# Four tokens to a partition for the keys and queries of two tiles, and a changed opening, in a sliding-window attention and feed-forward kernel

## The chip, the cores and the metric

The kernel runs on one core of a Trainium2 chip. The metric is device time in microseconds (us), the median of the runs; lower is better. The core has a matrix engine (TensorE, PE in the profile, with its weight loads as PEld), a vector engine (VectorE, DVE), a scalar engine (ScalarE, ACT), a general engine (GpSimd, POOL), and a queue engine (SyncE, SP). They work through their own instruction lists in order and wait for each other with semaphores. Transfers between the large memory and the on-chip memory (SBUF) run on 16 DMA engines; here SP, ACT and POOL issue them. TensorE writes to eight PSUM banks, from which VectorE and ScalarE read.

## What is computed

Eight batches of 576 tokens with 8 heads of 64 numbers go through attention in a window of 32 tokens to either side; the result, 4608 tokens of 512 numbers, goes through two dense layers with an activation between them:

```python
scores = scale * np.matmul(q, k.transpose(0, 1, 3, 2))
mask = np.abs(pos[:, None] - pos[None, :]) <= 32
attn = softmax(np.where(mask, scores, -1e9))
x = np.matmul(attn, v).transpose(0, 2, 1, 3).reshape(4608, 512)
h = x @ w_in                                  # 512 x 2048
g = h * (1.0 / (1.0 + np.exp(-1.702 * h)))
out = g @ w_out                               # 2048 x 512
```

Inputs and output are float32; inside, the kernel works in 16 bits.

## The kernel before

The 4608 tokens are taken as one row of 36 units of 128 queries, four units to a tile of 512, nine tiles in all. The queries are shifted by 32 tokens against the keys, so that a unit needs three blocks of 64 keys and two blocks of 64 queries. The transposed keys stand in `kT`, a ring of 1024 tokens; the transposed queries in `qT`, two tiles of four units.

`scores(u)` makes 24 products of 64 keys against 64 or 128 queries into two PSUM banks, and one exp on ScalarE turns all 1024 columns into `p`. In the first tile a negative mask is added on TensorE beforehand (two products of 128x512); later units are masked by VectorE after the exp (`band`). `values(u)` multiplies `p` with the values, which VectorE or POOL first copies with a shift of 64 tokens into `vo` (`odd_v`), `norm(u)` divides by the sums, and `x_T(u)` transposes the result into `xT` for the dense layers.

The order of the work is written out by hand: each engine executes its instructions in the order of the calls. `head()` does the first tile (units 0 to 3), the dense layers of these units (`layer1`, `layer2`), and the attention of unit 4 to 6; `pairs()` does units 7 to 11; from then on `step(T)` handles one tile at a time in a fixed order (`STEP`, `FIRST`). In `head()` all loads stand ahead of the computation, so POOL issues them in this order as fast as it can; it converts float32 to 16 bits on the way. Three loads (the first 128 keys and the first two units of queries) go through SP as float32, and VectorE and ScalarE round them (`load_raw`, `round_raw`).

Keys and queries of tiles 0 to 2 are loaded by `load_units` (L148): a partition holds one token, 8 heads of 64 numbers each, one transfer for each unit of 128 tokens and each batch that it touches. `transpose_units` makes four 128x128 products from each unit, and `put_units` copies the PSUM bank into `kT` (VectorE) or `qT` (ScalarE). For tile 1 `both_T` (L215) does two units of keys and queries in one double bank, between products of the second layer; for tile 2 `units_T` does the same between products of the first layer. From tile 3 on other functions do this, which stay as they are.

`keep_busy(n, kind)` (L579) issues n products of 128x256 on zeros into the named bank; nobody reads their result. It stands where TensorE would otherwise be idle. A bank named "o", "t", "h" or "i" exists once, "d" is a double bank and exists twice; a write to a bank waits until its last reader is done.

Of the kernel before, what the change touches and what calls it, by code (L numbers as in the profile page):

```python
# [33 lines left out]
class _Kernel:  # L34
# [110 lines left out]
            yield at - lo, b, s, m  # L145
            at += m

    def load_units(self, c, i, units, half=None):  # L148

        if (c, i) not in self.stage:  # L150
            tag, bufs = (("c2", 2), ("qs", 2), ("qs", 2))[i] if c == "q" else (("gs3", "gs1", "gs2")[i], 1)
            self.stage[c, i] = self.work.tile([128, 4, self.H, self.D], BF16, name=c + "s", tag=tag, bufs=bufs)
        src = {"q": self.q, "k": self.k}[c]
        for u in units:
            for n, (off, b, s, m) in enumerate(self.pieces(512 * i + 128 * u + (32 if c == "q" else 0), 128)):
                if half in (None, n):
                    self.nc.gpsimd.dma_start(self.stage[c, i][off:off + m, u], src[b, :, s:s + m, :].rearrange("h s d -> s h d"))

    def load_keys(self, i, units=range(4)):

# [45 lines left out]
            eng.tensor_copy(to, src)  # L206


    def units_T(self, c, i, units, kind, eng, n=128):

        tp = self.bank(kind, [128, len(units), 4, n], BF16, "tp")
        self.transpose_units(c, i, units, tp, n)
        self.put_units(c, i, units, tp, eng, n)

    def both_T(self, i, units, engs):  # L215

        tp = self.bank("d", [128, 2, 2, 4, 128], BF16, "tp")
        for n in range(2):
            self.transpose_units("kq"[n], i, units, tp[:, n])
        for n in range(2):  # L220
            self.put_units("kq"[n], i, units, tp[:, n], engs[n])

    def transpose_units(self, c, i, units, tp, n=128):
        for a, u in enumerate(units):
            for hp in range(4):
                self.nc.tensor.transpose(tp[:, a, hp, :], self.stage[c, i][:n, u, 2 * hp:2 * hp + 2, :], self.ident[:n, :n])  # L226

    def put_units(self, c, i, units, tp, eng, n=128):
        u, m = units[0], len(units)
        if c == "q":  # L230
            to = self.qT[:, :, i % 2, u:u + m]
        else:
            at = (512 * i + 128 * u) % RING
            to = self.kT[:, :, at:at + n * m].rearrange("r a (u p) -> r a u p", u=m)
        self.cast(eng, to, tp.rearrange("r u a p -> r a u p"))

    def load_raw(self, c, u, queue):
# [4 lines left out]
        queue.dma_start(raw, src[0, :, s0:s0 + 128, :].rearrange("h s d -> s h d"))  # L242

    def round_raw(self, c, u, eng):
        self.load_units(c, 0, ())
        self.cast(eng, self.stage[c, 0][:, u], self.stage.pop((c, "raw", u)))

    def scores(self, u, neg=None):
        nc = self.nc
        both, two = self.double("sc")  # L250
        for eo in range(2 if neg is not None else 0):
            nc.tensor.matmul(two[eo], self.ident, neg.rearrange("p h b s -> p (h b s)"), start=True, stop=False)
        sc = [t.rearrange("p (b s) -> p b s", s=SQ) for t in two]
        qT = self.qT[:, :, u // 4 % 2, u % 4].rearrange("r h (b s) -> r h b s", s=SQ)
        for hp in range(4):
            for chunk in range(3):
                lo, blks = 64 * (chunk % 2), slice(max(chunk - 1, 0), min(chunk, 1) + 1)
                at = 64 * (2 * u + chunk) % RING
                for eo in range(2):
                    r = slice(eo * 64, eo * 64 + 64)  # L260
                    nc.tensor.matmul(sc[eo][lo:lo + 64, 2 * hp + blks.start:2 * hp + blks.stop, :], self.kT[r, hp, at:at + 64],  # L261
                                     qT[r, hp, blks],
                                     start=neg is None and hp == 0 and chunk < 2, stop=hp == 3 and chunk > 0)
        p = self.work.tile([128, 2, 8, SQ], BF16, name="p", tag="p", bufs=4)
        nc.scalar.activation(p.rearrange("p e b s -> p e (b s)"), both, AF.Exp, scale=self.scale)  # L265
        self.p[u] = p

    def band(self, u, parts=2):
# [317 lines left out]
    def head(self):  # L586

        nc, dve, act, pool = self.nc, self.nc.vector, self.nc.scalar, self.nc.gpsimd
# [2 lines left out]
        act.copy(self.spark, self.spark)  # L591
        self.load_raw("k", 0, nc.sync)
        self.load_raw("q", 0, nc.sync)
        self.load_raw("q", 1, nc.sync)
        self.setup()
        self.load_units("q", 0, ())
        for u in (1, 2):
            self.load_units("k", 0, (u,))
        self.setup_mask()
        for m in range(3):  # L600
            self.load_v(m)
        self.load_units("k", 0, (3,))
        for u in (2, 3):
            self.load_units("q", 0, (u,))
# [32 lines left out]
        self.units_T("k", 0, (0,), "h", dve)  # L637
# [64 lines left out]
        run(2)  # L702
        self.band(4)
        self.scores(5)
        run(2)
        self.band(5)
        self.values(4)
# [41 lines left out]
    def pairs(self):  # L749

        nc, dve, act, pool = self.nc, self.nc.vector, self.nc.scalar, self.nc.gpsimd

        def run(lst, n=1):
            for _ in range(min(n, len(lst))):
                lst.pop(0)()
# [205 lines left out]
```

## Time and profile before

| | |
|---|---|
| median of 3 runs | 293.88 us (293.29 to 294.08) |
| profiled execution | 294.34 us, of which the span of the profile is 292.6 us |
| TensorE busy | 280.1 us (96%) |
| VectorE, ScalarE, POOL busy | 200.4, 201.9, 131.3 us |
| first run of first-layer products starts | 22.74 us |
| transposes of tile 1, of tile 2 | from 40.16 us, from 58.09 us |
| packets of POOL's loads | 114,208 |

The profile shows one execution. A line of its timeline gives the start, the duration, the engine, the source line, the operation, what it writes and reads with the shapes, how many there are, and in brackets how long the engine sat idle before it and what released it. A line of the windows gives for a stretch of time the length, the busy time and number of instructions of PE, PEld, DVE, ACT and POOL, the share of full speed that TensorE's clock was granted, the share of DMA, and GB/s.

### The profile page before, as it was taken

How to read it: one execution, taken by the hardware profiler on the slowest of the kernel's cores; microseconds unless marked ns; L12 is line 12 of the kernel's file. 1: busy time of each engine (PE TensorE's matmuls, PEld its weight loads, DVE VectorE, ACT ScalarE, POOL GpSimd, SP SyncE). 2: the span in 40 equal slices, each digit the busy share in tenths (PEclk: the TensorE clock that was granted, in tenths of full speed). 3: DMA queues.
4: the chain of work that ended last, by engine and by line, in shares of the span. 5: the costliest groups of instructions: out<-in, count | busy, mean ns of one | idle time of the engine just before them, and what ended most of it. 6: DMA issues, size and time to landing. Idle time of an engine off the chain costs nothing.

```text
span 292.6 us, 8655 instructions
## 1 busy us (share of the span) xinstructions
PE 280.1 (96%) x3601; PEld 225.4 (77%) x3601; DVE 200.4 (68%) x410; ACT 201.9 (69%) x303; POOL 131.3 (45%) x195
## 2 busy tenths in 40 slices
PE   5899999999999999999999999999999999999994
PEld 3568855786866768888788888888888788888884
DVE  2565426888848569777887787778767877737742
ACT  2475616689595779768976897689768975756830
POOL 8975789877772388359239618602100000000000
PEclk9799999999999999999999999999999999999999
DMA  9999999999999999999999999982503020300223
GB/s 138 156 196 204 162 186 156 209 174 120 157 116 151 128 157 134 125 151 156 227 119 161 199 167 139 132 148 90 74 0 145 20 58 0 147 0 2 80 102 108
DMA packets 158310, 37.26 MB, mean 127 GB/s; under 512 B 148544, under 2 KB 154176, under 8 KB 158272
## 3 DMA queue, kind: packets, MB, share of 16 engines
q0 software_dynamic: 114208, 17.97, 95.7%
q1 hardware_dynamic: 41984, 15.21, 32.1%
q10 hardware_dynamic: 2080, 3.54, 3.6%
q8 instruction: 28, 0.46, 0.7%
q14 instruction: 10, 0.08, 0.1%
HBM read 36.70 MB, written 9.44 MB: 158 GB/s over the span
## 4 chain that ended last, share of the span: by engine, by line
PE 72%; ACT 16%; DVE 6%; issue 2%; DMA 2%; SPq 0%; ACTq 0%
PE h_ps L424 28%; PE o_ps L495 20%; PE h_ps L335 8%; PE o_ps L347 7%; ACT p L265 7%; ACT g L430 3%; PE pv L294 3%; ACT L265 2%; PE tp L226 2%; DMA q_raw<-in_q_dram 2%; ACT L577 2%; DVE vo L206 2%; PE sc L261 2%; DVE x L307 1%; DVE p L278 1%
## 5 line engine op out<-in xcount | busy, mean ns | idle before, releaser
L424 PEld LDWEIGHTS <-w_in_s 128*128 128x128 f16 x448 | 42.7, 98 | 9.8 <-issue 2.9
L430 ACT ACTIVATE g<-h_ps 128x512 f16<-128x512 f32 x49 | 29.2, 595 | 28.4 <-PE h_ps L424 26.7
L495 PEld LDWEIGHTS <-g 128*128 128x128 f16 x448 | 43.4, 98 | 5.2
L265 ACT ACTIVATE p<-sc 128x1024 bf16<-128x1024 f32 x36 | 35.3, 1029 | 4.8 <-PE sc L261 4.5
L424 PEld LDWEIGHTS <-w_in_sb 128*128 128x128 f16 x336 | 32.6, 98 | 7.3 <-issue 0.6
L186 POOL DMA_DIRECT2D qu<-in_q_dram x30 | 24.0, 813 | 30.9 <-DMA qT<-qu 28.9
L495 PEld LDWEIGHTS <-gs 128*128 128x128 f16 x336 | 32.8, 98 | 4.2
L459 DVE TENSOR_TENSOR c<-h_ps,c 128x512 f32<-128x512 f32 x28 | 19.2, 686 | 22.8 <-PE h_ps L424 19.8
L196 POOL DMA_DIRECT2D ve<-in_v_dram x40 | 34.0, 869 | 0.4 <-PE pv L294 0.4
L430 ACT ACTIVATE g<-c 128x1024 f16<-128x1024 f32 (+1 forms) x35 | 34.0, 970 | 0.0
L424 PE MATMUL h_ps<-xT,w_in_s 128*128 128x256 f16 x224 | 33.6, 272 | 0.0
L424 PE MATMUL h_ps<-xT,w_in_sb 128*128 128x256 f16 x224 | 32.4, 272 | 0.3
L347 PE MATMUL o_ps<-w_out_sb,g 128*128 128x512 f16 x128 | 32.6, 380 | 0.0
L424 PE MATMUL h_ps<-xs,w_in_s 128*128 128x256 f16 x224 | 31.8, 272 | 0.6
L206 POOL COPY vo<-ve 64x264 int32<-64x264 int32 x49 | 22.1, 451 | 21.8 <-PE pv L294 15.6
L495 PE MATMUL o_ps<-w_out_s,g 128*128 128x256 f16 x224 | 31.5, 273 | 0.0
L335 PE MATMUL h_ps<-xT,w_in_sb 128*128 128x256 f16 x256 | 30.1, 273 | 0.6 <-DVE xT L129 0.6
L495 PE MATMUL o_ps<-w_out_s,gs 128*128 128x256 f16 x224 | 29.5, 272 | 0.0
L164 POOL DMA_DIRECT2D ks<-in_k_dram x27 | 22.8, 860 | 14.1 <-PE h_ps L424 4.8
L335 PEld LDWEIGHTS <-w_in_sb 128*128 128x128 f16 x256 | 24.3, 98 | 3.8 <-DVE xT L129 0.8
L495 PE MATMUL o_ps<-w_out_sb,g 128*128 128x256 f16 x224 | 26.6, 273 | 0.0
L337 ACT ACTIVATE g<-h_ps 128x512 f16<-128x512 f32 x32 | 18.9, 596 | 10.3 <-PE h_ps L335 10.3
(88 smaller groups left out, 473.8 us busy)
## 6 DMA issues: line engine op xcount, KB each, us to landing
ve<-in_v_dram POOLq DMA_DIRECT2D x32, 128.0 KB, 6.3
ks<-in_k_dram POOLq DMA_DIRECT2D x31, 128.0 KB, 7.1
out_dram<-o_sb SPq DMA_DIRECT2D x6, 512.0 KB, 2.9
out_dram<-o_sb ACTq DMA_DIRECT2D x6, 512.0 KB, 3.7
out_dram<-o_sb SPq DMA_DIRECT2D x9, 256.0 KB, 5.4
qu<-in_q_dram POOLq DMA_DIRECT2D x18, 128.0 KB, 7.3
w_out_sb<-in_moe_w_out_dram POOLq DMA_DIRECT2D x4, 512.0 KB, 8.8
w_in_sb<-in_moe_w_in_dram POOLq DMA_DIRECT2D x3, 512.0 KB, 8.2
```

The source lines that it names most:

```text
L164: self.nc.gpsimd.dma_start(ks[off:off + n], self.k[b, :, s:s + n, :].rearrange("h s d -> s h d"))
L186: self.nc.gpsimd.dma_start(qu[off:off + n], self.q[b, :, s:s + n, :].rearrange("h s d -> s h d"))
L196: self.nc.gpsimd.dma_start(self.ve[m % NV][off:off + n, :, :self.D], self.v[b, :, s:s + n, :].rearrange("h s d -> s h d"))
L206: eng.tensor_copy(to, src)
L265: nc.scalar.activation(p.rearrange("p e b s -> p e (b s)"), both, AF.Exp, scale=self.scale)
L335: nc.tensor.matmul(hps[:, i, :], self.w_in_sb[:, kr, ff * 128:(ff + 1) * 128], xT[:, kr, :], start=(i == 0 and kr == 0), stop=(i == 1 and ...
L337: nc.scalar.activation(g[:, 2 * d:2 * d + 2, :], hps, AF.Gelu_apprx_sigmoid)
L347: nc.tensor.matmul(o_ps, g[:, ff, s * 128:(s + 1) * 128], self.w_out_sb[:, ff, :], start=(ff == 0), stop=(ff == self.NFF - 1))
L424: nc.tensor.matmul(ps[:, i, :], a[:, kr, (2 * j + i) * 128:(2 * j + i + 1) * 128], x[:, kr, :], start=first and i == 0 and kr == 0, stop=i ...
L430: act.activation(out, src, AF.Gelu_apprx_sigmoid)
L459: dve.tensor_add(c22, ps, c22)
L495: nc.tensor.matmul(out, a[:, kb, p * 128:p * 128 + 128], b[:, kb, :], start=first and n in (0, 2 * two) and kb == 0, stop=n in (3, 3 - 2 * ...
```

## The change

Keys and queries of tiles 1 and 2 are loaded with four neighbouring tokens to a partition, so that a row of 4 x 64 numbers of one head is moved at once; a tile takes two transfers for keys and two for queries, since it touches two batches. Each head and each of the four tokens is then transposed by itself, 128x64, into the lower or upper half of a bank. The copy into `kT` puts the keys back in the order of the tokens; the queries stay in the order (token within four, group of four), `scores` picks them with a stepped pattern, and the exp restores the order of its columns. The 64 keys that unit 3 needs from tile 1 are loaded by themselves (`load_edge`, `edge_T`).

In the opening the second unit of queries is no longer loaded by SP but by POOL, second in its queue; POOL's first shift of values moves ahead of a weight load; there are more idle products; and the order of some transposes, products and shifts is another. Two transposes in `pairs()` change places.

```diff
-    def load_units(self, c, i, units, half=None):
...
+    def load_units(self, c, units):
...
+    def load_heads(self, i, c, heads=None):
+        key = (c, i)
+        if key not in self.stage:
+            tag, bufs = ("qs", 2) if c == "q" else (("gs1", "gs2")[i - 1], 1)
+            self.stage[key] = self.work.tile([128, self.H, JT * self.D], BF16, name=c + "s", tag=tag, bufs=bufs)
+        lo, hi = heads or (0, self.H)
         src = {"q": self.q, "k": self.k}[c]
...
+        for off, b, s, m in self.pieces(512 * i + (32 if c == "q" else 0), 512):
+            self.nc.gpsimd.dma_start(self.stage[key][off // JT:(off + m) // JT, lo:hi, :],
+                                     src[b, lo:hi, s:s + m, :].rearrange("h (p j) d -> p h (j d)", j=JT))
...
+    def heads_T(self, c, i, hps, kind, eng):
+        tp = self.bank(kind, [128, len(hps), JT, 128], BF16, "tp")
+        for a, hp in enumerate(hps):
+            for j in range(JT):
+                for t in range(2):
+                    self.nc.tensor.transpose(tp[64 * t:64 * t + 64, a, j, :],
+                                             self.stage[c, i][:, 2 * hp + t, j * self.D:(j + 1) * self.D], self.ident)
+        to = slice(hps[0], hps[-1] + 1)
+        if c == "q":
+            self.cast(eng, self.qT[:, to, i % 2], tp)
+            return
+        at = 512 * i % RING
+        self.cast(eng, self.kT[:, to, at:at + 512].rearrange("r a (p j) -> r a p j", j=JT), tp.rearrange("r a j p -> r a p j"))
...
+    def load_edge(self):
+        self.stage["edge"] = self.work.tile([64, self.H, self.D], BF16, name="edge", tag="x", bufs=5)
+        self.nc.gpsimd.dma_start(self.stage["edge"], self.k[0, :, 512:576, :].rearrange("h s d -> s h d"))
...
     def scores(self, u, neg=None):
...
+        mixed = 4 <= u < 12
+        if mixed:
+            qT = self.qT[:, :, u // 4 % 2].rearrange("r h j (b s) -> r h b j s", s=16)
+            b0 = u % 4 * 2
...
-                                     qT[r, hp, blks],
+                                     qT[r, hp, b0 + blks.start:b0 + blks.stop],
...
+        if mixed:
+            nc.scalar.activation(p.rearrange("p e b (r j) -> p (e b) r j", j=JT),
+                                 both.rearrange("p e (b j r) -> p (e b) r j", j=JT, r=16), AF.Exp, scale=self.scale)
...
     def head(self):
...
-        self.load_raw("q", 1, nc.sync)
         self.setup()
-        self.load_units("q", 0, ())
-        for u in (1, 2):
-            self.load_units("k", 0, (u,))
+        self.load_units("q", ())
+        self.load_units("k", (1,))
+        self.load_units("q", (1,))
+        self.load_units("k", (2,))
...
-        self.load_units("k", 1, (0,), 0)
+        self.load_edge()
         self.load_v(3)
         self.load_w_in(0, 1)
+        self.load_w_in(1, 2)
         self.load_v(4, 0)
-        self.load_w_in(1, 2)
+        self.odd_v(2, pool)
         self.load_w_in(2, 4)
-        self.odd_v(2, pool)
...
-        self.load_units("k", 1, (0,), 1)
-        self.load_units("q", 1, (0,))
         for c in "kq":
-            self.load_units(c, 1, (1,))
-        for u in range(2, 4):
-            for c in "kq":
-                self.load_units(c, 1, (u,))
+            self.load_heads(1, c)
...
-        for u in range(4):
-            for c in "kq":
-                self.load_units(c, 2, (u,))
+        for c in "kq":
+            self.load_heads(2, c)
...
-        self.keep_busy(2, "o")
-        self.units_T("q", 0, (0,), "o", act)
-        self.keep_busy(2, "i")
-        self.units_T("k", 0, (1,), "t", dve)
-        self.round_raw("q", 1, act)
-        self.keep_busy(2, "i")
+        self.keep_busy(6, "o")
+        self.units_T("q", (0,), "o", act)
+        self.keep_busy(4, "i")
+        self.units_T("k", (1,), "t", dve)
+        self.units_T("q", (1,), "h", act)
+        self.keep_busy(3)
         self.scores(0, self.neg)
-        self.units_T("k", 0, (2,), "h", dve)
-        self.units_T("q", 0, (1,), "o", dve)
-        self.keep_busy(3, "t")
+        self.units_T("k", (2,), "o", dve)
+        self.keep_busy(5, "t")
+        self.scores(1, self.neg)
         self.odd_v(0, dve)
-        self.scores(1, self.neg)
+        self.keep_busy(2, "t")
         self.values(0, "ot")
         self.odd_v(1, dve)
         self.norm(0)
-        self.keep_busy(2, "h")
+        self.keep_busy(4, "h")
         self.values(1, "hh")
-        self.units_T("q", 0, (2,), "d", act)
-        self.units_T("k", 0, (3,), "d", dve)
+        self.keep_busy(2)
+        self.x_T(0, "o", act)
+        self.units_T("k", (3,), "d", dve)
+        self.units_T("q", (2,), "d", act)
         self.norm(1)
-        self.x_T(0, "o", act)
+        self.keep_busy(2, "o")
         self.scores(2, self.neg)
-        self.units_T("q", 0, (3,), "t", act)
-        self.units_T("k", 1, (0,), "o", dve, 64)
+        self.units_T("q", (3,), "t", act)
+        self.edge_T("o", dve)
...
-        run(6)
-        self.both_T(1, (0, 1), (dve, act))
-        run(1)
-        self.both_T(1, (2, 3), (dve, act))
+        run(5)
+        for hps in ((0, 1), (2, 3)):
+            self.heads_T("k", 1, hps, "d", dve)
+            self.heads_T("q", 1, hps, "d", act)
+            run(2)
         for m in (4, 5):
             self.odd_v(m, dve)
+        self.scores(4)
         run(1)
-        self.scores(4)
-        run(2)
+        self.scores(5)
         self.band(4)
-        self.scores(5)
...
         for hps in ((0, 1), (2, 3)):
-            self.units_T("k", 2, hps, "t", dve)
-            self.units_T("q", 2, hps, "o", act)
+            self.heads_T("k", 2, hps, "t", dve)
+            self.heads_T("q", 2, hps, "o", act)
...
+        self.keys_PE(3, 1, "o", act)
         self.x_T(9, "t", dve)
-        self.keys_PE(3, 1, "o", act)
```

More of the change, by code (lines that the diff above doesn't have):

```diff
@@ L146, in pieces @@
             at += m
-    def load_units(self, c, i, units, half=None):
-        if (c, i) not in self.stage:
-            tag, bufs = (("c2", 2), ("qs", 2), ("qs", 2))[i] if c == "q" else (("gs3", "gs1", "gs2")[i], 1)
-            self.stage[c, i] = self.work.tile([128, 4, self.H, self.D], BF16, name=c + "s", tag=tag, bufs=bufs)
+    def load_units(self, c, units):
+        if (c, 0) not in self.stage:
+            tag, bufs = ("c2", 2) if c == "q" else ("gs3", 1)
+            self.stage[c, 0] = self.work.tile([128, 4, self.H, self.D], BF16, name=c + "s", tag=tag, bufs=bufs)
+        src, at = {"q": (self.q, 32), "k": (self.k, 0)}[c]
+        for u in units:
+            s = at + 128 * u
+            self.nc.gpsimd.dma_start(self.stage[c, 0][:, u], src[0, :, s:s + 128, :].rearrange("h s d -> s h d"))
+    def load_heads(self, i, c, heads=None):
[4 more added lines that the diff above has]
+        lo, hi = heads or (0, self.H)
         src = {"q": self.q, "k": self.k}[c]
[L154 to L157, printed above, removed]
+        for off, b, s, m in self.pieces(512 * i + (32 if c == "q" else 0), 512):
+            self.nc.gpsimd.dma_start(self.stage[key][off // JT:(off + m) // JT, lo:hi, :],
+                                     src[b, lo:hi, s:s + m, :].rearrange("h (p j) d -> p h (j d)", j=JT))
     def load_keys(self, i, units=range(4)):
@@ L206, in odd_v, with units_T @@
             eng.tensor_copy(to, src)
[L209 to L223, printed above, removed]
+    def heads_T(self, c, i, hps, kind, eng):
[11 more added lines that the diff above has]
+        self.cast(eng, self.kT[:, to, at:at + 512].rearrange("r a (p j) -> r a p j", j=JT), tp.rearrange("r a j p -> r a p j"))
+    def units_T(self, c, units, kind, eng):
+        n = len(units)
+        tp = self.bank(kind, [128, n, 4, 128], BF16, "tp")
         for a, u in enumerate(units):
             for hp in range(4):
-                self.nc.tensor.transpose(tp[:, a, hp, :], self.stage[c, i][:n, u, 2 * hp:2 * hp + 2, :], self.ident[:n, :n])
-    def put_units(self, c, i, units, tp, eng, n=128):
-        u, m = units[0], len(units)
+                self.nc.tensor.transpose(tp[:, a, hp, :], self.stage[c, 0][:, u, 2 * hp:2 * hp + 2, :], self.ident)
+        u = units[0]
         if c == "q":
-            to = self.qT[:, :, i % 2, u:u + m]
+            to = self.qT[:, :, 0, u:u + n]
         else:
-            at = (512 * i + 128 * u) % RING
-            to = self.kT[:, :, at:at + n * m].rearrange("r a (u p) -> r a u p", u=m)
+            to = self.kT[:, :, 128 * u:128 * (u + n)].rearrange("r a (u p) -> r a u p", u=n)
         self.cast(eng, to, tp.rearrange("r u a p -> r a u p"))
@@ L244, in round_raw, with edge_T @@
     def round_raw(self, c, u, eng):
-        self.load_units(c, 0, ())
+        self.load_units(c, ())
         self.cast(eng, self.stage[c, 0][:, u], self.stage.pop((c, "raw", u)))
+    def load_edge(self):
+        self.stage["edge"] = self.work.tile([64, self.H, self.D], BF16, name="edge", tag="x", bufs=5)
+        self.nc.gpsimd.dma_start(self.stage["edge"], self.k[0, :, 512:576, :].rearrange("h s d -> s h d"))
+    def edge_T(self, kind, eng):
+        nc = self.nc
+        src = self.stage["edge"]
+        tp = self.bank(kind, [128, 4, 64], BF16, "tp")
+        for hp in range(4):
+            nc.tensor.transpose(tp[:, hp, :], src[:, 2 * hp:2 * hp + 2, :], self.ident[:64, :64])
+        self.cast(eng, self.kT[:, :, 512:576], tp)
     def scores(self, u, neg=None):
@@ L253, in scores @@
         sc = [t.rearrange("p (b s) -> p b s", s=SQ) for t in two]
-        qT = self.qT[:, :, u // 4 % 2, u % 4].rearrange("r h (b s) -> r h b s", s=SQ)
+        mixed = 4 <= u < 12
+        if mixed:
+            qT = self.qT[:, :, u // 4 % 2].rearrange("r h j (b s) -> r h b j s", s=16)
+            b0 = u % 4 * 2
+        else:
+            qT, b0 = self.qT[:, :, u // 4 % 2, u % 4].rearrange("r h (b s) -> r h b s", s=SQ), 0
         for hp in range(4):
@@ L261, in scores @@
                     nc.tensor.matmul(sc[eo][lo:lo + 64, 2 * hp + blks.start:2 * hp + blks.stop, :], self.kT[r, hp, at:at + 64],
-                                     qT[r, hp, blks],
+                                     qT[r, hp, b0 + blks.start:b0 + blks.stop],
                                      start=neg is None and hp == 0 and chunk < 2, stop=hp == 3 and chunk > 0)
         p = self.work.tile([128, 2, 8, SQ], BF16, name="p", tag="p", bufs=4)
-        nc.scalar.activation(p.rearrange("p e b s -> p e (b s)"), both, AF.Exp, scale=self.scale)
+        if mixed:
+            nc.scalar.activation(p.rearrange("p e b (r j) -> p (e b) r j", j=JT),
+                                 both.rearrange("p e (b j r) -> p (e b) r j", j=JT, r=16), AF.Exp, scale=self.scale)
+        else:
+            nc.scalar.activation(p.rearrange("p e b s -> p e (b s)"), both, AF.Exp, scale=self.scale)
         self.p[u] = p
@@ L601, in head @@
             self.load_v(m)
-        self.load_units("k", 0, (3,))
-        for u in (2, 3):
-            self.load_units("q", 0, (u,))
-        self.load_units("k", 1, (0,), 0)
+        self.load_units("k", (3,))
+        self.load_units("q", (2, 3))
+        self.load_edge()
         self.load_v(3)
         self.load_w_in(0, 1)
+        self.load_w_in(1, 2)
         self.load_v(4, 0)
-        self.load_w_in(1, 2)
+        self.odd_v(2, pool)
         self.load_w_in(2, 4)
-        self.odd_v(2, pool)
         self.load_w_in(4, 6)
@@ L636, in head @@
         self.round_raw("q", 0, act)
-        self.units_T("k", 0, (0,), "h", dve)
+        self.units_T("k", (0,), "h", dve)
         self.negative_mask()
-        self.keep_busy(2, "o")
-        self.units_T("q", 0, (0,), "o", act)
-        self.keep_busy(2, "i")
-        self.units_T("k", 0, (1,), "t", dve)
-        self.round_raw("q", 1, act)
-        self.keep_busy(2, "i")
+        self.keep_busy(6, "o")
[4 more added lines that the diff above has]
+        self.keep_busy(3)
         self.scores(0, self.neg)
-        self.units_T("k", 0, (2,), "h", dve)
-        self.units_T("q", 0, (1,), "o", dve)
-        self.keep_busy(3, "t")
+        self.units_T("k", (2,), "o", dve)
+        self.keep_busy(5, "t")
+        self.scores(1, self.neg)
         self.odd_v(0, dve)
-        self.scores(1, self.neg)
+        self.keep_busy(2, "t")
         self.values(0, "ot")
```

## The prediction

> **What bounds the kernel now.** I read the page's busy line and clock line first, then the windows of the first 25 us, the timeline of the opening, and the chain of waits.
>
> ```profile
> PE 280.1 (96%) x3601; PEld 225.4 (77%) x3601; DVE 200.4 (68%) x410; ACT 201.9 (69%) x303; POOL 131.3 (45%) x195
> PEclk9799999999999999999999999999999999999999
> ```
>
> TensorE is busy in 280.1 of 292.6 us at full clock, but for one dip in the second slice. What can be won without taking products away lies where it idles or runs slowly: the first 20 us.
>
> ```profile
> 0.00:5.00 5.00, 3.47 (x20) 2.28 (x20) 1.33 (x14) 1.47 (x2) 4.05 (x13) 1.00 0.67 118
> 5.00:10.00 5.00, 2.80 (x17) 1.59 (x14) 1.05 (x3) 1.72 (x3) 5.00 (x7) 0.74 2.12 167
> 10.00:15.00 5.00, 4.02 (x98) 2.90 (x98) 3.68 (x9) 2.05 (x2) 4.78 (x7) 0.92 2.19 159
> ```
>
> The columns are PE, PEld, DVE, ACT, POOL, then the clock. Five microseconds at 0.74 and five at 0.92 are together 3.4 us at half clock; the trace's clock records put them at 7.4 to 10.8. Before that TensorE idles from 5.2 to 7.4, for the first queries:
>
> ```profile
> 1.35 1.55 SPq L242 DMA_DIRECT2D q_raw<-in_q_dram  x2
> ...
> 6.75 0.62 ACT L129 CAST qs<-q_raw 128x512 bf16<-128x512 f32 x1 [4.45 <-DMA q_raw<-in_q_dram]
> ...
> 7.42 0.61 PE L226 MATMUL tp<-ident,qs 128*128 128x128 bf16 x4 [2.20 <-ACT qs L129]
> ...
> 9.10 1.06 PE L252 MATMUL sc<-neg,ident 128*128 128x512 bf16 x2
> ...
> 11.95 2.54 DVE L206 COPY vo<-ve 64x528 bf16<-64x528 bf16 x4
> ...
> 18.99 1.02 ACT L265 ACTIVATE p<-sc 128x1024 bf16<-128x1024 f32 x1 [0.53 <-PE sc L261]
> ```
>
> Everything up to the first long run of first-layer products (22.74) hangs on that cast and then passes through the shifted values (vo), norm(0) and the fourth exp (18.99). The second stretch with slack is 50 to 94 us, where the chain goes through VectorE and ScalarE:
>
> ```profile
> 61.37 0.69 DVE L129 COPY kT<-tp 128x1024 bf16<-128x1024 bf16 x1 [0.75 <-PE tp L226]
> ...
> 65.50 2.85 ACT L265 ACTIVATE p<-sc 128x1024 bf16<-128x1024 f32 x3
> ...
> 66.56 0.69 DVE L278 TENSOR_TENSOR p<-p,mask 128x1024 bf16<-128x1024 bf16 x1 [0.58 <-ACT p L265]
> ```
>
> After 94 us the products run nearly without gaps, and no load ends a wait of TensorE after the opening.
>
> **The loads, tile 1 and 2.** 17 issues of keys and queries (0.87 us each on POOL) become 8, plus one for the 64 edge keys; 16,384 packets of 128 B become 4,096 of 512 B. In the trace 128 B packets move 0.154 MB per us, the weights' larger ones 0.205, so 2.1 MB takes 10.2 instead of 13.6 us, less 0.4 for the edge: DMA is some 3 us ahead. Worth on the path: nothing direct, because tile 1 landed at 37.9 and its transposes ran at 40.16, tile 2's landed by 53 for 58.09. Indirectly the shifted values at 53.68 (0.58 and 0.55, with POOL issuing; 0.29 at best) may be quicker, and they are on the chain: I take -0.2, bounds 0 and -0.5.
>
> **Their transposes.** 16 of 64 columns replace 8 of 128, eight times. The value products have that shape (128x64) and start in pairs, 16 in 0.25 us, so two take the time of one: I take 0. If they did not pair, 64 more at 0.056 us: +3.6.
>
> **The key copies** read every 128th element. A 128x1024 bf16 copy takes 0.69, 128x512 bf16 0.42, 128x512 f32 0.69: unpaired elements cost 1.04 ns, hence 1.22 us, +0.53 four times. Tile 1: VectorE had been idle for 8.65 us and its next mask product waits 1.71 us for ScalarE; hidden. Tile 2: the 0.75 and 0.58 us of idle time in the fence above take both; hidden, and +1.06 if that cover were gone. If stepped reading also halves the rate: +1.07 each, about +1.0 on the chain.
>
> **Scores and exps of units 4 to 11.** The moving operand comes in runs of 16, the exp reads PSUM at a step of 16. No row here reads so. Nearest: ScalarE takes 1.01 us for 1024 bf16 and 1.02 for 1024 f32, so it goes by elements; I take 0. Bounds: nothing; or half rate, 8 x 0.85 for the exps (4.3 on the chain, five in the run from 65.5) and 8 x 0.37 for the scores. The Trainium skill, "Advanced Engine Details and Errata", section Memory Cachelines, says that every two neighbouring PSUM elements should be contiguous, and that other patterns slow matmuls; it names no price for an exp. By it the last rival below is the forecast.
>
> **The opening.** Offsets from the queries' cast, 6.75. Four transposes take 0.22 at full clock, an idle product 0.11, the two mask products 0.46, scores 0.37, and a reader starts 0.2 after the last product. Now: first exp at 4.04, vo from 5.20, norm(0) done 8.82, fourth exp 12.24. With full clock after the change: transposes 0.67 to 0.89, four idle products 1.33, keys 1.55, queries(1) 1.77, three idle 2.10, mask 2.56, scores 2.93, exp 3.13; keys(2) 3.15, their copy 3.36 to 3.78; vo 3.78 to 6.32, norm(0) 7.55. That is 1.3 better. But then x_T(0), which needs norm(0), stands ahead of the transposes of keys(3) and queries(2), which ran at 14.88 while norm(0) was still going. So: x_T(0) ends 7.75, those transposes 8.20, ScalarE copies x_T(0) until 8.54, then the queries until 9.13; two idle products wait for that first copy; scores(2) 9.22 to 9.59, third exp 9.79 (now 10.21), the copy of queries(3) behind it to 11.40, scores(3) to 11.82, fourth exp 12.02 against 12.24. Of 1.3 us, 0.2 stays. POOL issues queries(1) besides, so the values are issued 0.88 later; v1 lands between 10.2 (the queue goes on at 0.84 us a load) and 11.5 (issue plus 5.2 as now), and the second vo copy wants it at 11.2: cost 0 to 0.3, I take 0.1. POOL's shift of values 2 moves ahead of a 512 KB weight load, which then waits for v3 (landing 15.3); it would land at about 21.4 as now and is needed at 24.5: nothing.
>
> **When the queries land** decides. Of the sixteen completion marks of that load fifteen arrive by 5.10 and one at 6.70, while POOL's first keys come in. Removing the third raw load leaves those keys; I take 6.75 again, with 5.3 as the other end.
>
> **The clock.** 20% busy in 4.0 to 7.4 lost it. The change makes that about a third (six idle products for two). I take it as kept. The Trainium skill, "TensorE: Matmul & The Clock Gate", section Why this matters for your kernels, asks only that no gap be over about 3 us; the trace's gap of 2.2 us lost it all the same, so the measurement decides and the rule gives no comfort.
>
> **Sum:** -0.2 + 0.1 (opening) - 0.2 (vo at 53) = -0.3 us. The profiled execution took 294.34 with a span of 292.6 (1.7 around it), 0.46 over the median of the runs: 294.0 by its own time, 293.6 by the median 293.88.
>
> **Rivals.**
> *Queries land at 5.3.* For it: fifteen engines did. Against: the late one competed with POOL's keys, which stay. Then the values bind: v1 at 10.25, two more copies to 12.2, norm(0) 13.4, fourth exp 17.9 instead of 18.99: -1.1, with the vo gain -1.3: 292.6.
> *The clock is lost all the same.* Then idle products stand on the path: from 0.65 to 4.05 after the cast everything takes double: transposes 1.12, four idle 1.98, keys and queries 2.86, three idle 3.51, mask 4.24, scores 4.61, vo from 5.46 instead of 3.78; plus the later order: fourth exp +1.5: 295.2. It decides as soon as the clock falls before the first scores.
> *Stepped reading is slow* (exps, scores, copies or unpaired transposes): +1.0 for the copies alone, +4.3 for the exps: 295 to 298, middle 297. Against: the elementwise ScalarE rows.
> *The load packing helps more than I see* would need a wait for a load on the chain; the trace has none after 20 us.
>
> **Numbers.** Forecast 32%, early queries 28%, lost clock 22%, slow stepping 18%. The measurement can tell about 0.3%, 0.88 us, from no change. Faster: 27 of the second case and 6 from the forecast's low end, 33%; same: 22 of the forecast, 1 of early queries and 2 of lost clock, 25%; slower: 4 + 20 + 18 = 42%. The forecast's own range is 293.0 to 294.5; to leave out no more than 2 in 10 it must take in most cases of both signs: 292.0 to 296.8.
>
> **What would show it.** Right: the queries' cast near 6.7, no clock below 1.0 in 5 to 15 us, vo from about 10.5, but x_T(0) ahead of the late transposes and a fourth exp near 18.8; exps of units 4 to 11 at 1.02, key copies at 1.2, sixteen transposes in 0.45. Wrong: a cast before 6; clock 0.74 again; exps above 1.1 us; VectorE's chain from 66.56 starting later against TensorE's scores(7).

## The result, and the profile after

The changed kernel took 294.93 us (median of 12 runs, 294.20 to 295.82), the kernel before 293.34 (12 runs on the same chip, 291.79 to 294.08). The ratio is 1.0064, 95% interval 1.0045 to 1.0084: slower by 1.3 to 2.5 us, where 0.3 us less was forecast.

The two profiles that stand side by side don't show this: their spans are 292.6 and 292.5 us. The page of before is one of its longer executions (294.34), that of after the shortest of its twelve (294.20). First, the page of after, busy line and clock line, and two rows of its windows (columns as before: length, PE, PEld, DVE, ACT, POOL, clock, DMA share, GB/s):

```profile
PE 281.5 (96%) x3680; PEld 225.8 (77%) x3682; DVE 201.2 (69%) x409; ACT 201.9 (69%) x303; POOL 124.7 (43%) x186
PEclk9999999999999999999999999999999999999999
```

```profile
5.00:10.00 5.00, 4.62 (x86) 3.39 (x86) 1.86 (x5) 2.81 (x4) 4.95 (x8) 1.00 1.82 116
10.00:15.00 5.00, 3.78 (x55) 2.34 (x55) 2.85 (x11) 2.19 (x3) 4.99 (x7) 1.00 2.20 145
```

The dip of the clock is gone, POOL works 6.6 us less, and TensorE 1.4 us more: 64 transposes and 17 idle products were added. Now the timeline of after, with the lines that answer to those shown of before:

```profile
5.21 0.62 ACT L129 CAST qs<-q_raw 128x512 bf16<-128x512 f32 x1 [2.92 <-DMA q_raw<-in_q_dram]
...
5.89 0.40 PE L241 MATMUL tp<-ident,qs 128*128 128x128 bf16 x4 [0.24 <-ACT qs L129]
...
8.34 1.02 ACT L299 ACTIVATE p<-sc 128x1024 bf16<-128x1024 f32 x1 [0.55 <-PE sc L291]
...
15.50 1.02 ACT L299 ACTIVATE p<-sc 128x1024 bf16<-128x1024 f32 x1 [0.67 <-PE sc L291]
...
17.53 1.02 ACT L299 ACTIVATE p<-sc 128x1024 bf16<-128x1024 f32 x1 [0.53 <-PE sc L291]
...
62.18 1.22 DVE L129 COPY kT<-tp 128x1024 bf16<-128x1024 bf16 x1 [0.44 <-PE tp L226]
...
66.41 2.85 ACT L296 ACTIVATE p<-sc 128x1024 bf16<-128x1024 f32 x3
...
67.47 0.69 DVE L312 TENSOR_TENSOR p<-p,mask 128x1024 bf16<-128x1024 bf16 x1 [0.56 <-ACT p L296]
```

The queries' cast is 1.54 us earlier than in the page of before, the first exp 2.45, the fourth 1.46; the run of first-layer products that started at 22.74 starts at 22.49. Between the first exp and this run 2.2 us of the lead are lost. The chain of waits of after, up to that run, shows where (start, duration, what):

```profile
5.48 2.60 POOL ve L207 x3
8.07 0.87 POOL ks L156
8.95 1.83 POOL qs L156 x2
10.77 0.73 POOL edge L263
11.51 0.87 POOL ve L207
12.38 1.46 POOL w_in_sb L133 x2
13.84 5.68 DMA ve<-in_v_dram
19.51 0.05 issue
19.56 0.41 POOL vo L217
19.98 0.04 issue
20.02 0.42 PE pv L328 x15
...
22.49 1.59 PE h_ps L369 x13
```

It no longer goes through the cast, the exps or TensorE, but through POOL's list of loads, one issue after the other, to the first half of values 4. That half is issued at 13.84, behind two weight loads, and lands at 19.51; POOL's shift for unit 3 waits for it, and values(3) on TensorE for the shift. In the waits of TensorE in the first 24 us of after this is the largest but for the start:

```profile
PE junk L617 <- DVE idle L98: 1.2, 1, 1.2
PE pv L328 <- POOL vo L217: 1.0, 1, 1.0
```

A second profile of each kernel is from the experiments (e4 and e16, the kernel before and the changed one once more); the last column is experiment e14. Times in us:

| | before | before, e4 | after | after, e16 | after with its loads put back, e14 |
|---|---|---|---|---|---|
| queries' cast | 6.75 | 5.27 | 5.21 | 5.19 | 5.22 |
| first exp | 10.79 | 8.65 | 8.34 | 9.05 | 8.70 |
| third exp | 16.96 | 14.94 | 15.50 | 15.70 | 14.87 |
| run of 112 products | 22.74 | 21.01 | 22.49 | 22.59 | 20.89 |
| ratio to before | 1 | 0.9992 | 1.0064 | 1.0069 | 0.9999 |

Beside e4 the changed opening is 1.5 us late. In the kernel before, too, the queries can land by 5.3, and the dip of the clock is not in every execution: of the 142 runs of before that stand beside the experiments, 28 have a mean granted clock of 0.995 or less, as the page of before has (0.994). Of the 1.70 us between the starts of e16 and e14, 1.64 are left at the table load near 110 us (112.53 and 110.89).

### The profile page after: what moved, and what is told of

Same layout as the page of the kernel before. It is cut to its first block, busy times and chain, and to the rows that moved or that the text cites. A ratio compares the mean times of both kernels' runs of the same rounds, so it can differ in the third digit from the quotient of the medians.

```text
span 292.5 us, 8798 instructions
## 1 busy us (share of the span) xinstructions
PE 281.5 (96%) x3680; PEld 225.8 (77%) x3682; DVE 201.2 (69%) x409; ACT 201.9 (69%) x303; POOL 124.7 (43%) x186
## 4 chain that ended last, share of the span: by engine, by line
PE 68%; ACT 17%; DVE 5%; POOL 4%; issue 3%; DMA 2%; ACTq 0%; POOLq 0%; DVEq 0%
PE h_ps L458 28%; PE o_ps L529 20%; PE h_ps L369 8%; ACT p L299 7%; PE o_ps L381 6%; ACT g L464 3%; ACT L299 2%; ACT L611 2%; DMA ve<-in_v_dram 2%; DVE p L312 2%; PE pv L328 2%; DVE x L341 1%; PE tp L226 1%; POOL ve L207 1%; POOL ks L156 1%
## 5 line engine op out<-in xcount | busy, mean ns | idle before, releaser
L217 POOL COPY vo<-ve 64x264 int32<-64x264 int32 x49 | 23.4, 477 | 18.7 <-DMA ve<-in_v_dram 9.9
L299 ACT ACTIVATE p<-sc 128x1024 bf16<-128x1024 f32 x28 | 27.4, 1030 | 2.5 <-PE sc L291 2.4
```

## The experiments

Each was timed in turn with the kernel before, 12 runs each (e1, e7 and e16 rest on 6, e15 on 9). "Start" means the start of the run of 112 first-layer products.

### The two halves of the change (e1, e2, e4), and the first suspect (e3)

e1 is the new opening with the old loads of tiles 1 and 2; e2 the old opening with the new loads, transposes, scores and exps of these tiles (and `load_edge`, `edge_T`, and the two places changed in `pairs()`); e4 the kernel before, unchanged. e3 is the changed kernel with

```diff
-        self.load_w_in(1, 2)
         self.load_v(4, 0)
-        self.odd_v(2, pool)
+        self.load_w_in(1, 2)
         self.load_w_in(2, 4)
+        self.odd_v(2, pool)
```

> The new opening alone; keys and queries of tiles 1 and 2 loaded and transposed as before. Theory O (the loss lies in the opening: half of values 4 lands behind a weight load and the fourth unit's values wait for its shift): +0.8 to +1.6 us against before, the 112-product run of the first layer later than before's, scores of unit 4 no later relative to it. Theory M (the loss lies in tiles 1 and 2: later scores(4) and slower transposes): within 0.5 us of before or faster.

> The old opening (three raw loads by SP, fewer idle products, old order), but keys and queries of tiles 1 and 2 four tokens to a partition, with the edge keys loaded in place of the half unit. Theory M: +0.5 to +1.2 us against before, the profile showing 1.0 for 32 transposes against 0.89 for 16 and the exp of unit 4 waiting for its table. Theory O: within 0.5 us of before.

> The changed kernel with the half of values 4 issued ahead of the second weight load and POOL's first shift behind the third, as before. Theory O: 0.6 to 1.2 us faster than the changed kernel, the half landing near 18 us instead of 19.5 and values(3) starting right after the fourth exp (18.8 us). Theory M: no more than 0.3 us faster than the changed kernel, as tiles 1 and 2 are unchanged.

> The kernel before once more, for a second profile of it and a check of the spread. If the shown profile (294.34 us) was a slow one of its kind: first queries cast before 6.0 us and no clock below 1.0, the first-layer run starting 0.7 to 1.2 us earlier than 22.74. If it was typical: cast near 6.7 us and a dip of the clock again.

Measured: e1 296.78 us, ratio 1.0143 (1.0099 to 1.0187); e2 293.50, 1.0019 (0.9999 to 1.0038); e3 294.28, 1.0039 (1.0014 to 1.0063); e4 292.78, 0.9992 (0.9967 to 1.0016). The loss lies in the opening. Alone it costs 4.2 us by its ratio, more than the whole change and more than either theory had. The order of the half of values 4 is part of it, not all. In e3 that half is no longer what TensorE waits for, but the second group of first-layer products then waits 0.27 us for the weight load behind it (w_in(1,2)), and the run of 112 starts at 22.51, no earlier than in after; the profile is of one of e3's longer runs (295.35), with the cast at 6.04.

The chain of waits of e1 shows what follows when POOL is late and tile 1 still takes its many issues:

```profile
13.64 6.39 DMA ve<-in_v_dram
20.03 0.05 issue
20.08 0.40 POOL vo L206
...
22.65 12.24 DMA w_out_sb<-in_moe_w_out_dram
34.89 0.28 issue
35.18 0.88 POOL ks L157
...
39.95 8.52 DMA ve<-in_v_dram
48.47 0.02 issue
48.50 0.04 DVE vo L206
```

The same shift is late (20.08), the weight loads behind it are, and at 34.89 POOL stands until one of them has landed: from 23 us on, in this profile as in that of e4, the load that POOL waits for stands eight places ahead in its list. So lateness in the opening is handed on to the values 5 and 6, and VectorE's shift of values 5 waits for them until 48.5. With the packed loads POOL has fewer issues there.

### The parts of the opening, alone in the kernel before (e5, e6, e10, e8, e12)

```diff
 e5, POOL's order
-        self.load_v(4, 0)
         self.load_w_in(1, 2)
+        self.load_v(4, 0)
+        self.odd_v(2, pool)
         self.load_w_in(2, 4)
-        self.odd_v(2, pool)
 e6, x_T(0) first
+        self.x_T(0, "o", act)
+        self.units_T("k", 0, (3,), "d", dve)
         self.units_T("q", 0, (2,), "d", act)
-        self.units_T("k", 0, (3,), "d", dve)
         self.norm(1)
-        self.x_T(0, "o", act)
 e10, second queries by POOL
-        self.load_raw("q", 1, nc.sync)
...
         self.load_units("k", 0, (1,))
+        self.load_units("q", 0, (1,))
         self.load_units("k", 0, (2,))
...
-        self.round_raw("q", 1, act)
 e12, the first two groups of idle products (e8: all groups of the change)
-        self.keep_busy(2, "o")
+        self.keep_busy(6, "o")
         self.units_T("q", 0, (0,), "o", act)
-        self.keep_busy(2, "i")
+        self.keep_busy(4, "i")
```

> The kernel before with one edit in POOL's queue, as the change has it: the weight load w_in(1,2) ahead of the first half of values 4, and the shift of values 2 ahead of the weight load w_in(2,4). Theory A (the half of values 4 now lands behind a weight load, POOL's shift for unit 3 waits for it, and values(3) on TensorE waits for that shift): POOL's wait for the half of values 4 ends about 19 to 20 us instead of 17, the run of 112 first-layer products starts 0.6 to 1.5 us later than the 21.0 of the kernel before, total +0.5 to +1.2 us. Rival B (the order of x_T(0) or the later loads cost it, not this): start within 0.3 us of 21.0, total within 0.5 us of before.

> The kernel before with one edit on TensorE: x_T(0) ahead of the transposes of keys(3) and queries(2), as the change has it. Theory A (TensorE stands at x_T(0) until norm(0) is done, and the third and fourth exp come later): third exp 0.4 to 0.6 us later than 14.94, fourth the same than 16.96; but values(3) had 0.6 us or more of slack behind the shift of values, so the run of 112 products moves by 0 to 0.5 us and the total by +0 to +0.5 us. Rival B (the whole loss is here): run of 112 products +1 us or more, total +1 us or more.

> The kernel before with one edit: the second queries loaded by POOL, second in its queue, not by SP. Theory A (each later load of POOL is issued 0.87 us later, the transposes of queries(2) and keys(3), the shifts of values 2 and 3 wait for them): third exp 0.5 to 1.5 us later than 15.0 to 16.2 of the other runs with this opening, run of 112 products at 22.3 to 23.5, total +0.8 to +2 us. Rival B (these loads have slack): total within 0.5 us of before.

> The kernel before with the change's idle products alone (6, 4 and 3 ahead of the first scores, 5 and 2 ahead of the second and of values 0, 4, 2 and 2 later). In six profiles with the old opening TensorE's products up to the first scores took 0.61 us for four transposes, that is half rate, in three (until 9.4 to 11 us), 0.40 in the others; in four profiles with the change's opening they were never slow after 5.7. Theory A (the idle products keep the rate): four transposes of the queries take 0.40, the first exp comes 2.6 to 3.4 us after the queries' cast, total 0 to 0.8 us under before. Rival B (they are only in the way): the first exp 3.4 us or more after the cast, total +0.2 us or more.

> The kernel before with only the first two groups of idle products longer, 6 and 4 instead of 2 and 2. Theory A (these are the ones that bring TensorE to its full rate ahead of the first scores): as the run with all of them, total 0.2 to 0.9 us under before, the fastest of all. Rival B (the rate at the start doesn't reach the run of 112 products, since the loads of queries(2) and values come later than it): total within 0.2 us of before.

| | edit | start | us | ratio (95%) |
|---|---|---|---|---|
| e5 | POOL's order | 21.83 | 294.06 | 1.0042 (1.0016 to 1.0069) |
| e6 | x_T(0) first | 21.93 | 293.29 | 1.0002 (0.9978 to 1.0027) |
| e10 | second queries by POOL | 22.56 | 294.69 | 1.0047 (1.0024 to 1.0071) |
| e8 | all idle products | 20.97 | 294.74 | 1.0048 (1.0018 to 1.0078) |
| e12 | 6 and 4 idle products | 20.80 | 293.68 | 1.0007 (0.9983 to 1.0030) |

e5 and e10 cost what their theory A said (though the third exp of e10, at 15.26, is not late), and e6 nothing. The parts add up within their intervals: 0.42 + 0.02 + 0.47 + 0.48 = 1.39%, beside 1.43% for the whole opening in e1. What TensorE waits for differs. In e5 it is POOL's shift of the half of values 4 (0.85 us at 19.36), and no run separates the two moves of that edit, the weight load and the shift. In e10 the first two groups of first-layer products wait for their weight loads, which are as late as everything else in the list:

```profile
18.62 1.05 PE L335 MATMUL h_ps<-xT,w_in_sb 128*128 128x256 f16 x8 [0.43 <-DMA w_in_sb<-in_moe_w_in_dram]
...
20.44 1.05 PE L335 MATMUL h_ps<-xT,w_in_sb 128*128 128x256 f16 x8 [0.40 <-DMA w_in_sb<-in_moe_w_in_dram]
```

e8 fits neither theory whole: its transposes take 0.40, as theory A wanted; its first exp comes 3.46 us after the cast and its total is later, as rival B had it; but the opening is level with e4's (start 20.97 against 21.01), so the idle products are not in the way there. VectorE's shift of values 5 waits for a load at 46 us (timeline), 0.86 later than in e4, but at the table load near 110 us the two are level again (110.18 and 110.11). Behind it an exp is waited for (waits of TensorE), and the last copy of VectorE comes 0.9 later than in e4:

```profile
46.42 0.34 DVE L206 COPY vo<-ve 64x528 bf16<-64x528 bf16 x1 [3.27 <-DMA ve<-in_v_dram]
```

```profile
PE h_ps L424 <- ACT p L265: 1.8, 1, 1.8
```

e12 has the first of these too (2.66 us at 45.97), and no loss. Four of e8's twelve runs have a mean granted clock of 0.994 and took 295.14 to 297.10; the median of the eight others is 294.48. What makes the 0.48% of e8 is open.

### The parts of the opening, inside the changed kernel (e7, e11, e14, e15, e16)

e7 is e3 with the transposes of keys(3) and queries(2) back ahead of x_T(0). e11 is the changed kernel with the second queries by SP again and transposed behind keys(2); e14 is e11 with the edit of e3 as well, so that all loads of the opening are issued as before; e15 is the changed kernel with the idle products of before; e16 is the changed kernel itself.

> The changed kernel with both edits undone: the half of values 4 ahead of w_in(1,2), the shift of values 2 behind w_in(2,4), and x_T(0) behind the transposes of keys(3) and queries(2). Theory A (these two are what the changed opening loses): run of 112 products at 20.7 to 21.3 us instead of 22.5, total 293.2 to 293.8, that is what the loads of tiles 1 and 2 cost alone. Rival B (the second queries by POOL make every load behind them 0.9 us later, and that alone holds values(3)): run of 112 products at 21.8 or later, total 294.2 or more.

> The changed kernel with the second queries loaded by SP again, and transposed behind keys(2) as before; all else as changed. Theory A (the load moved to POOL is what makes the changed opening late): POOL issues values 0 at 4.6 instead of 5.4, run of 112 products at 21.5 to 22.0 instead of 22.5, total 293.6 to 294.2, 0.7 to 1.3 under the changed kernel. Rival B (the order of POOL's later work is the whole loss): total 294.4 or more.

> The changed kernel with both edits of the opening's loads undone: the second queries by SP (transposed behind keys(2)), and the half of values 4 ahead of w_in(1,2) with the shift of values 2 behind w_in(2,4). Theory A (these two are the loss, and they add: alone each undo gave 0.7): total 0.0 to 0.6 us over before, run of 112 products at 20.8 to 21.6 us. Rival B (the larger part is the idle products and the order of x_T(0)): total 1.0 us or more over before.

> The changed kernel with the idle products of the kernel before (2, 2, 2, 3 and 2, none at the new places). Theory A (in the kernel with the old loads all idle products together cost 1.4 us, so they stand in the way here too): total 0.5 to 1.5 us under the changed kernel. Rival B (TensorE's rate falls without them, and what they cost alone came from later waits that the packed loads lift): total as the changed kernel or up to 1 us over it, products up to the first scores at half rate.

> The changed kernel again, to stand beside the other runs of this set: 294.3 to 295.2, ratio 1.004 to 1.008, run of 112 products at 22.0 to 23.0 us.

| | undone in the changed kernel | start | us | ratio (95%) |
|---|---|---|---|---|
| e16 | nothing | 22.59 | 295.17 | 1.0069 (1.0042 to 1.0095) |
| e15 | idle products | 22.43 | 295.33 | 1.0068 (1.0043 to 1.0093) |
| e11 | second queries by POOL | 21.89 | 294.19 | 1.0033 (1.0014 to 1.0053) |
| e14 | that and POOL's order | 20.89 | 293.08 | 0.9999 (0.9981 to 1.0017) |
| e7 | POOL's order and x_T(0) | 25.65 | 296.65 | 1.0118 (1.0075 to 1.0161) |

e14 settles it: the two edits of the opening's loads (the first with the place of the transposes of these queries) are the whole loss, 1.0069 - 0.9999 = 0.70%, some 2 us; each undone alone (e3, e11) gives back about a half. The idle products cost nothing in the changed kernel (e15). POOL's timeline in e16, and then in e14, shows the same three instructions, first values, half of values 4, shift for unit 3:

```profile
5.42 2.69 POOL L207 DMA_DIRECT2D ve<-in_v_dram  x3
...
13.78 0.73 POOL L207 DMA_DIRECT2D ve<-in_v_dram  x1
...
19.66 0.40 POOL L217 COPY vo<-ve 64x264 int32<-64x264 int32 x1 [1.14 <-DMA ve<-in_v_dram]
```

```profile
4.56 2.65 POOL L207 DMA_DIRECT2D ve<-in_v_dram  x3
...
12.19 0.72 POOL L207 DMA_DIRECT2D ve<-in_v_dram  x1
...
17.40 0.41 POOL L217 COPY vo<-ve 64x264 int32<-64x264 int32 x1 [0.20 <-DMA ve<-in_v_dram]
```

The half of values 4 is issued 1.59 us later in e16: 0.86 for the second queries in front of everything (5.42 against 4.56), 0.73 for the weight load that went ahead. The shift is 2.26 us later, the start 1.70.

e7 was a miss: theory A expected the start at 21, and it came at 25.65, in the range of rival B but not for its reason. x_T(0) ahead of the two transposes had been put down as a loss; with the loads late it is a cover. Without it TensorE stands at queries(2), and its clock falls (timeline, then two rows of the windows):

```profile
14.96 0.40 PE L241 MATMUL tp<-ident,qs 128*128 128x128 bf16 x4 [2.26 <-DMA qs<-in_q_dram]
```

```profile
10.00:15.00 5.00, 2.69 (x66) 1.76 (x66) 1.95 (x7) 1.02 (x1) 5.00 (x7) 1.00 2.14 144
15.00:20.00 5.00, 4.33 (x52) 2.85 (x53) 1.70 (x6) 2.26 (x4) 2.44 (x6) 0.53 1.38 171
```

The lost clock is the larger part, and it is not in every run. Three of the six, this profile among them, took 297.65 to 297.94 at a mean granted clock of 0.987 or 0.988; the other three took 295.12 to 295.65 at 0.992 to 1.000, about 1 us over the median of e3.

### Is there a version that beats both? (e9, e13, e18, e17)

e2 makes nine groups of four second-layer products (`run(1)`, in the expectations a pair) ahead of scores(4), where before has eight. e9 is e2 with

```diff
-        run(5)
+        run(6)
         for hps in ((0, 1), (2, 3)):
...
-            run(2)
+            run(1)
...
         self.scores(4)
-        run(1)
+        run(2)
         self.scores(5)
```

e13 and e18 (the same kernel twice) are e9 with the 6 and 4 idle products of e12; e17 is e14 with the order of e9.

> The kernel before with the new loads, transposes, scores and exps of tiles 1 and 2 alone, and with scores(4) behind eight pairs of second-layer products as before, not nine. Theory A (the packed loads' own cost of about 0.5 us is the later scores(4): the activation table of the fifth exp and the exp wait for it, and the exps after it follow; behind it the quicker shifts of values give back about 0.9 us): fifth exp 0.6 to 0.9 us earlier, against the start of the 112 products, than with the change's order, and total 0.5 to 0.9 us under before. Rival B (the cost is the stepped key copies and the 64-column transposes): total as with the change's order, 0 to +0.8 us over before.

> The kernel before with the packed loads of tiles 1 and 2, scores(4) at its old place, and the first two groups of idle products at 6 and 4; the opening is otherwise the old one. Theory A (an earlier opening is lost at 46 us in the kernel with the old loads, because the shift of values 5 waits there for the half of values 6, and the packed loads lift that wait): the first exps come as early as in the run with the idle products alone, the shift of values 5 waits for no load beyond 45.5, and the total is 0.4 to 1.2 us under before. Rival B (what bounds 46 to 60 us is VectorE's own work, and the packed loads' slow key copies add to it): total within 0.4 us of before or over it.

> The fastest kernel so far again (packed loads, scores(4) at its old place, first two groups of idle products at 6 and 4, all loads of the opening as before): ratio to before 0.997 to 1.000. If it is over 1.000, its win of 0.3 us in the set before was chance.

> The changed kernel with both edits of the opening's loads undone and scores(4) at its old place, behind eight pairs of second-layer products. Theory A (the later scores(4) costs what the trace shows between the start of the 112 products and the fifth exp, 24.1 us and more against 23.4): fifth exp 0.5 to 0.9 us earlier against that start than with the loads back alone, total 0.3 to 0.9 us under before. Rival B (VectorE's masks and the table load behind 60 us set the pace, and an earlier fifth exp is only a longer wait): total within 0.3 us of before.

Measured: e9 293.34 us, 1.0007 (0.9987 to 1.0027); e13 292.79, 0.9986 (0.9970 to 1.0002); e18 292.78, 0.9994 (0.9976 to 1.0012); e17 292.90, 0.9995 (0.9978 to 1.0012). The fifth exp comes earlier as wanted (44.76 in e17, 46.16 in e14), but the total moves by 0.04%, less than the intervals can tell. From the start of the 112 products to the table load near 110 us it is 90.00 us in e14 and 88.97 in e17, but 88.92 in e2 and 89.33 in e9, so neither order is the shorter in both pairs. In e14 a part of it is that TensorE, which comes to the transposes one group earlier there, waits for the packed queries of tile 1:

```profile
39.09 0.64 PE L226 MATMUL tp<-ident,qs 128*64 128x128 bf16 x16 [0.91 <-DMA qs<-in_q_dram]
```

The shift of values 5 starts earlier in e13 (45.01 against 45.97 in e12), and still none of the four is told apart from the kernel before. The packed loads neither win nor lose.

## Why the prediction was wrong, step by step

**The step that failed** is the one on POOL's list in the opening. "POOL issues queries(1) besides, so the values are issued 0.88 later [...] I take 0.1": 0.86 was right, but it was followed only as far as values 1. Everything behind it is late too, and what can't wait there are the half of values 4 and the weight load beside it in the list, w_in(1,2). Whichever goes second is waited for: the half of values 4 in e5, e16 and after (0.85 to 1.01 us), the weight load in e4, e14, e12, e3 and e10 (0.18 to 0.40). Alone the 0.86 cost 0.47% (1.4 us, e10). "POOL's shift of values 2 moves ahead of a 512 KB weight load [...] nothing": what the shift passes was priced, and what the other move of that edit passes was not. w_in(1,2) went ahead of the half of values 4, and the edit with both moves, alone in the old kernel, cost 0.42% (1.2 us, e5). Together, inside the changed kernel, the two steps were worth 0.70% (2 us) where the sum had 0.1. The page of before held a warning: in its timeline the same shift, at 17.82, had waited 1.00 us for that load. It cost nothing there, since values(3) needed the shift only at 20.24.

**"I take 6.75 again"** read one execution as the kernel. Eight profiles with the idle products of before have the cast at 5.19 to 6.75, twelve with those of the change at 5.17 to 6.65. The cast moves from run to run with either, and the issues in POOL's list don't move with it.

**"Of 1.3 us, 0.2 stays"**, because of x_T(0) ahead of the transposes: in the kernel before this order costs nothing (e6, 1.0002), and in the changed one it saves time (e7 against e3). The walk through the opening followed TensorE, ScalarE and VectorE and left out that the loads of keys(3) and queries(2) set this place (in after the transposes of keys(3) wait 0.40 us for theirs and start 13.59 - 5.21 = 8.38 after the cast, where 7.75 was forecast).

**The offsets in front of that** were right: the first exp was forecast 3.13 us after the cast, and came 3.13 after it (8.34 - 5.21). So was **the clock** in this page: kept, no idle product on the path of the first exp. In e16 full rate came only at 6.73 us, behind the first six idle products, and the exp 3.86 after the cast. It wins nothing, because the run of 112 waits for POOL's loads (in the old kernel too: start 20.80 in e12, 21.01 in e4).

**The tiles.** Forecast -0.2 us, measured +0.2 and +0.6 (ratios 1.0007 in e9 and 1.0019 in e2, both with 1 in the interval). The parts were mostly sized well. The stepped key copy takes 1.22 us (forecast 1.22). The stepped exps take 1.02 as the others do, 1023 ns against 1030 in the groups; the rule of the Trainium skill that was weighed there ("Advanced Engine Details and Errata", Memory Cachelines) shows in none of these exps. Transposes do pair: 32 of 64 columns run from 39.13 to 40.15, 16 of 128 in e4 from 38.43 to 39.32, so each of the four groups costs 0.13 us more, not 0.9; the forecast put this 0.5 us at nothing. The two shifts near 53 us took 0.98 us on average in the eight profiles with the old loads and 0.77 in the twelve with the packed ones, the 0.2 that was forecast. POOL's issues for the two tiles fell from 18 to 8 (17 was a miscount), but DMA was not "some 3 us ahead": in e14 the packed queries of tile 1 land at 38.95, where the old loads had landed by 37.9, and TensorE waits for them. That scores(4) stands one group later was not seen, and cost nothing that could be measured (e17 against e14).

**The rivals.** The queries did land at 5.2, and the fourth exp came at 17.53, where that rival had 17.9; but its 292.6 did not follow, since the lead was lost behind that exp, and since a cast at 6.75 was not the rule before. Lost clock and slow stepping didn't happen in the two profiles of the changed kernel. The rival that was missing is the one that came true: POOL's list of loads as the bound, with the half of values 4 as its point in the changed kernel. What was the bound of the page, a late cast and a low clock, hid it.

**Still open:** why all idle products alone cost 0.48% in the kernel with the old loads, and nothing in the one with the packed ones; and which of the two moves of e5 costs how much.

## What to carry to other kernels

Where one queue issues all loads in order, price an edit by the first load behind it that somebody waits for, however far down the list, and do it for what is passed as well as for what passes. Before the shown bound of a stretch is taken as the kernel's, ask whether it is in every execution: a landing time that fifteen of sixteen marks contradict is a sample. Where two loads that are needed at about the same time stand next to each other, price both orders: changing their places changes which of them is waited for, and here (e5) the wait grew. And a reorder that looks like a loss in one kernel can be cover in another, so undo parts inside the changed kernel, not only in the old one.

## What the runs showed of the hardware

**The rate of TensorE at the start isn't the granted clock of the page.** With 2 and 2 idle products in the first two groups, the two mask products ahead of the first scores took 1.0 us or more, about half rate, in five of eight profiles; with 6 and 4 they took 0.59 in twelve of twelve. The windows of e10 grant a clock of 1.00 there all the same: the clock records of its trace begin only at 10.48 us, those of e8 at 3.96, and the windows show 1.00 for what lies before the first record. In all twenty traces the products change to the higher rate where the records begin: with 6 and 4 at 3.86 to 6.97 us; with 2 and 2 at 4.01 to 5.75 in four (in the page of before the clock is lost again at 7.43) and at 9.47 to 10.48 in four. The timelines of e10 and of e8, from the queries' transposes to the mask:

```profile
5.86 0.61 PE L226 MATMUL tp<-ident,qs 128*128 128x128 bf16 x4 [0.23 <-ACT qs L129]
...
7.54 1.06 PE L252 MATMUL sc<-neg,ident 128*128 128x512 bf16 x2
```

```profile
5.87 0.40 PE L226 MATMUL tp<-ident,qs 128*128 128x128 bf16 x4 [0.24 <-ACT qs L129]
...
7.66 0.59 PE L252 MATMUL sc<-neg,ident 128*128 128x512 bf16 x2
```

The Trainium skill, "TensorE: Matmul & The Clock Gate", section Part 1: The HAM clock gate (the "warmup" mystery), puts the switch to full rate at about 4 us of sustained products, in windows that run freely, so that it varies by 0.5 us from run to run. No run here has 4 us of sustained products at the start: the first 14 take from 1.17 to about 4.3 us, and behind them TensorE is only partly busy. The traces agree that the switch varies, and here by more: with the same 14 products at the start it comes between 3.86 and 10.48 us.

**The end of the kernel varies from profile to profile.** From the table load near 111 us to the start of VectorE's last copy, eleven of twelve profiles with the packed loads take 177.5 to 177.6 us (one 179.4), but of eight with the old loads four take 178.5 to 179.3 and four 177.5 to 177.9. Where the time goes differs (a wait of 1.8 us for an exp in e8, two of 0.5 in e4). Why is not known, and so few profiles don't show that the loads at the beginning decide it; it means that a single span is uncertain by a us or more.
